# A two-block layer of convolution, token mix and channel mix: the token mix's sums taken for two blocks per instruction, with h1's columns reordered

## Chip, core and metric

One core of a Trainium2 chip runs the whole program. The metric is device time in microseconds (us) of one execution; the kernel before took 2136.81 us (median of two executions, 2135.29 and 2138.33).

## What is computed

```python
# x: 8 x 4096 x 192; weight: 8 heads x 7 taps
w = softmax(weight)                                     # over the 7 taps
xc[b, s, h, :] = sum_k w[h, k] * x[b, s + k - 6, h, :]   # causal convolution, 24 channels per head
h = relu(xc^T @ w_tok1) @ w_tok2                         # token mix: 4096 -> 256 -> 4096
u = xc + h^T
out = u + relu(u @ w_ch1) @ w_ch2                        # channel mix: 192 -> 1536 -> 192
```

All of it is float32 in and out. The matrix products are made of a high and a low part of each operand (three products per pair).

## The kernel before

The eight batches are taken in groups: batch 0, batch 1, and then three pairs (2,3), (4,5), (6,7). Each group has two stages. Stage 1 makes the convolution on ScalarE (first tap) and VectorE (other taps, line 667) and the first token product on TensorE, summed in PSUM; `mix1_done` (line 380) turns that sum into `h1`, the high part by ScalarE and the low part by VectorE. Stage 1 of a later group runs as background work: a planner (`Background`) keeps its own estimates of TensorE's and VectorE's time, and at every `bg.fg(pe, dve, after)` call in the foreground it places background instructions until its estimate for VectorE is `after` ns ahead of TensorE's. So the numbers given to `bg.fg` decide where taps stand on VectorE.

Stage 2 of a pair runs in units. A unit is one block of 512 tokens of both batches, that is two tiles, and there are eight units per pair, 24 in all. In the second tile of a unit the order on TensorE is: `channel1` (line 1077, six pairs of banks, evicted by line 1091 on ScalarE and line 1092 on VectorE), then `mix2` for the next unit (line 904), then the two halves of `channel2` (line 1119), then `channel1` of the next unit's first tile.

`mix2` for a pair makes four token blocks (`j` 0 to 3). Each is six matmuls of 384 columns (lines 930 to 932, h1's two batches of 192 columns side by side) into one bank of PSUM. Two blocks share one tile `two` of two banks; `banks()` hands out three such tiles in turn. After each block one VectorE add (line 936) reads the bank in u's order of columns (`p c b d`: block of 64 channels, batch, channel), while h1 has them as `b c d`, and adds it into `u`. Line 962 then transposes the block of `u` in 32x32 squares (`turn_blocks`). When all four blocks are turned, `blocks_sent` sends them to other partitions by 16 small DMAs (line 998, half on SyncE's queue and half on GpSimd's); then `release` lets the held background transfers go. `parted` splits what arrived into high and low (line 1011 ScalarE, line 1013 VectorE) and copies halves across (line 1016 ScalarE, line 1018 DMA). The next `channel1` reads these.

For batch 0's first tile `mix2` runs with `at_once`: four blocks of 18 small matmuls over both parts (lines 923 to 925), an add (line 942) and a copy (line 943) per block; here, too, two blocks share one two-bank tile. Batch 1 and the rest of batch 0 take the path of lines 927 and 953, which already adds two blocks at once.

Of the kernel before, what the change touches and what calls it, by code (L numbers as in the profile page):

```python
# [11 lines left out]
AF = mybir.ActivationFunctionType  # L12
ALU = mybir.AluOpType
# [126 lines left out]
def conv_mixer_kernel(ctx: ExitStack, tc: tile.TileContext, x, weight, w_tok1, w_tok2, w_ch1, w_ch2, out):  # L140
    nc = tc.nc
    B, S, D = x.shape
# [8 lines left out]
    D2 = P // 2  # L151
# [15 lines left out]
    def f32(ap):  # L167
        return ap.bitcast(F32)
# [7 lines left out]
    bg = Background()  # L176

    def banks():
        return ps_x.tile([P, 2, TT], F32, name="ps_x")
# [200 lines left out]
    def mix1_done(gi, accs):  # L380
        n = len(GROUPS[gi]) * D
        for kc in range(KC):
            a = accs[kc][:, :n]
            nc.scalar.activation(out=h1[:, kc, 0, :n], in_=a, func=AF.Relu)
            nc.vector.scalar_tensor_tensor(
                out=h1[:, kc, 1, :n], in0=a, scalar=0.0, in1=f32(h1[:, kc, 0, :n]), op0=ALU.max, op1=ALU.subtract
            )

    def mix1_accs():
        return [ps_a.tile([P, TT], F32, name=f"ps_a{kc}") for kc in range(KC)]  # L390
# [3 lines left out]
    def stage1_first(pe, p0, pd, late, load_u, load_next, after, thirds, hooks):  # L394
# [181 lines left out]
        for n in range(nj - 1):  # L576
# [10 lines left out]
            if n + 2 == nj:  # L587
                woven(chains[0][:1], chains[1][:1], split(n - 2))
                mix1_done(0, accs)
                woven(chains[0][1:])  # L590
                begin(n + 1)
                continue
# [39 lines left out]
    def stage1(gi, pools):  # L632
# [216 lines left out]
        def finish():  # L849
            bg.finish(gi)  # L850
            mix1_done(gi, accs)
# [44 lines left out]
    def rows(v):  # L896
        if len(v.shape) == 3:
            return v.rearrange("p j (c d) -> p j c d", d=D2)
        return v.rearrange("p (c d) -> p c d", d=D2)
# [4 lines left out]
    def mix2(gi, q, t2, u, at_once=False, turned=None, between=(), i=None):  # L904
        nb = len(GROUPS[gi])
        n = nb * D

        def lhs(kc, r, j):
            if gi:
                return t2[kc][:, r, j, :]  # L910
            a0 = ((q % 2) * TJ + j) * P
            return t2s[q // 2][:, kc, r, a0:a0 + P]

        for j in range(TJ):
            if j % 2 == 0:
                two = banks()
            ps = two[:, j % 2]
            for kc in range(KC):
                a, z = kc == 0, kc == KC - 1
                wh, wl = lhs(kc, 0, j), lhs(kc, 1, j)  # L920
                hh, hl = h1[:, kc, 0, :n], h1[:, kc, 1, :n]
                if at_once:
                    nc.tensor.matmul(out=ps[:, :D], lhsT=wh, rhs=hh, start=a, stop=False)
                    nc.tensor.matmul(out=ps[:, :D], lhsT=wh, rhs=hl, start=False, stop=False)
                    nc.tensor.matmul(out=ps[:, :D], lhsT=wl, rhs=hh, start=False, stop=z)
                elif nb == 1:
                    nc.tensor.matmul(out=ps[:, :2 * D], lhsT=wh, rhs=h1[:, kc, :, :n], start=a, stop=False)
                    nc.tensor.matmul(out=ps[:, :D], lhsT=wl, rhs=hh, start=False, stop=z)
                else:
                    nc.tensor.matmul(out=ps[:, :n], lhsT=wh, rhs=hh, start=a, stop=False)  # L930
                    nc.tensor.matmul(out=ps[:, :n], lhsT=wh, rhs=hl, start=False, stop=False)  # L931
                    nc.tensor.matmul(out=ps[:, :n], lhsT=wl, rhs=hh, start=False, stop=z)  # L932
            if nb > 1:
                bg.fg(1040, 532, 200)
                v = ps[:, :n].rearrange("p (b c d) -> p c b d", b=nb, d=D2)
                nc.vector.tensor_tensor(out=u[:, j], in0=v, in1=u[:, j], op=ALU.add)  # L936
                turn_blocks(u[:, j], turned, j)
                continue
            if at_once:
                bg.fg(570, 355, 200)  # L940
                one, two_ = u[:, j, :, 1], u[:, j, :, 0]
                nc.vector.tensor_tensor(out=two_, in0=rows(ps[:, :D]), in1=one, op=ALU.add)
                nc.scalar.copy(out=one, in_=two_)
                if j < len(between):
                    between[j]()
                continue
            bg.fg(570, 1110 if j % 2 else 0, 200)
            if j % 2 == 0:
                continue
            js = slice(j - 1, j + 1)  # L950
            one = u[:, js, :, 1 if i is None else i]
            total = u[:, js, :, 0] if i is None else one
            nc.vector.tensor_tensor(out=one, in0=rows(two[:, :, :D]), in1=one, op=ALU.add)
            nc.vector.tensor_tensor(out=total, in0=rows(two[:, :, D:2 * D]), in1=one, op=ALU.add)
            if i is None:
                nc.scalar.copy(out=one, in_=total)
            elif turned is not None:
                for k in (j - 1, j):
                    turn_blocks(u[:, k], turned, k)

    def turn_blocks(uj, turned, j):
        nc.vector.transpose(  # L962
            out=turned[:, :, j * QB:(j + 1) * QB],
            in_=uj.rearrange("p c b d -> p (c b d)").rearrange("p (n e) -> p n e", e=QB),
        )
        bg.dve += 580
# [69 lines left out]
    def first_mix(between):  # L1036
        mix2(0, 0, *first["u"], at_once=True, between=between)
# [206 lines left out]
    u = None  # L1244
# [9 lines left out]
    for gi, bs in enumerate(GROUPS):  # L1254
        nb = len(bs)
# [9 lines left out]
        if gi == 0:  # L1265
            u, abc = first["u"][1], first["abc"]
            loaded = first["next"]
        for n, unit in enumerate(units[gi]):
            nxt = (gi, n + 1) if n + 1 < len(units[gi]) else (gi + 1, 0)
            for i, (b, q) in enumerate(unit):  # L1270
# [27 lines left out]
                if turn and blocks:  # L1298
                    z = up.tile([P, ND * NQ, P], F32, name="own_hi")
                    t2, v = loaded  # L1300
                    if tiles:
                        for k in range(2 - len(t2), 2):
                            mix2(nxt[0], following[k][1], t2[k - 2], v, i=k, turned=z if k else None)
                    else:
                        mix2(nxt[0], nxt[1], t2[0], v, turned=z)
                    other = blocks_sent(z)
                    bg.release()
                elif turn:
                    if gi == 0 and nxt[0] == 0:
                        bg.require(("t2", nxt[1] // 2, nxt[1] % 2))  # L1310
                    mix2(*nxt, None, loaded[1])
                    mixed[0] = nxt[1]
                elif blocks and nxt[0] == gi and len(bs) == 1:
                    mix2(gi, following[0][1], loaded[0][0], loaded[1], i=0)
                    loaded = [load_t2(following[1][1], sp)], loaded[1]
# [27 lines left out]
                if turn:  # L1343
                    u = loaded[1]
# [33 lines left out]
```

## Time and profile before

| | |
|---|---|
| median of the two executions shown | 2136.81 us |
| the profiled execution | 2134.78 us, of which the span is 2133.0 us |
| TensorE busy | 2039.9 us (96%) |
| VectorE busy | 1410.8 us (66%) |
| ScalarE busy | 729.6 us (34%) |
| chain that ended last | 79% TensorE, 11% VectorE, 4% ScalarE |

The first unit's `mix2` for a pair begins at 610 us of the span, the last one's at 2056 us. In the names of the rows PE is TensorE's matmuls, PEld its weight loads, DVE VectorE, ACT ScalarE, POOL GpSimd, SP SyncE's queue. Matmuls overlap, so the distance from one start to the next is what one costs.

### The profile page before, as it was taken

How to read it: one execution, taken by the hardware profiler on the slowest of the kernel's cores; microseconds unless marked ns; L12 is line 12 of the kernel's file. 1: busy time of each engine (PE TensorE's matmuls, PEld its weight loads, DVE VectorE, ACT ScalarE, POOL GpSimd, SP SyncE). 2: the span in 40 equal slices, each digit the busy share in tenths (PEclk: the TensorE clock that was granted, in tenths of full speed). 3: DMA queues.
4: the chain of work that ended last, by engine and by line, in shares of the span. 5: the costliest groups of instructions: out<-in, count | busy, mean ns of one | idle time of the engine just before them, and what ended most of it. 6: DMA issues, size and time to landing. Idle time of an engine off the chain costs nothing.

```text
span 2133.0 us, 40820 instructions
## 1 busy us (share of the span) xinstructions
PE 2039.9 (96%) x17339; PEld 1868.5 (88%) x17339; DVE 1410.8 (66%) x2279; ACT 729.6 (34%) x863; POOL 240.9 (11%) x423
## 2 busy tenths in 40 slices
PE   9889999999999997999999999999999999999999
PEld 9779998899888897989888988998888889888788
DVE  7689876789858886856875689444445554445444
ACT  4564533334332332323333324223222232223222
POOL 0100001111111011101111110111110001111110
PEclk9999999999999999999999999999999999999999
DMA  9744537568454467234654334432221223223310
GB/s 316 253 144 153 172 105 193 160 180 230 115 175 113 138 177 192 78 90 132 161 148 115 96 107 136 139 82 80 80 62 53 59 74 80 80 73 80 80 38 23
DMA packets 294469, 264.61 MB, mean 124 GB/s; under 512 B 210512, under 2 KB 242768, under 8 KB 294288
## 3 DMA queue, kind: packets, MB, share of 16 engines
q1 hardware_dynamic: 268704, 169.57, 28.6%
q0 software_dynamic: 25584, 92.43, 14.5%
q8 instruction: 137, 2.24, 0.5%
q14 instruction: 44, 0.36, 0.1%
HBM read 146.60 MB, written 71.30 MB: 102 GB/s over the span
## 4 chain that ended last, share of the span: by engine, by line
PE 79%; DVE 11%; ACT 4%; issue 3%; DMA 2%; SPq 1%; POOL 0%; ACTq 0%; DVEq 0%; POOLq 0%
PE ps_x L1049 33%; PE ps_x L1108 15%; PE ps_x L1126 14%; PE ps_x L1127 6%; DVE xc L667 3%; DVE hl L1092 2%; ACT hh L1091 2%; PE ps_x L930 2%; DVE u L936 2%; PE ps_a L769 1%; PE ps_a L770 1%; PE ps_a L771 1%; PE ps_x L932 1%; PE ps_x L931 1%; PE ps_a L455 1%
## 5 line engine op out<-in xcount | busy, mean ns | idle before, releaser
L1091 ACT ACTIVATE hh<-ps_x 128x1024 fp32r<-128x1024 f32 x378 | 387.6, 1027 | 753.6 <-PE ps_x L1049 753.5
L1092 DVE SCALAR_TENSOR_TENSOR hl<-ps_x,hh 128x1024 fp32r<-128x1024 f32 x378 | 462.4, 1224 | 254.1 <-ACT hh L1091 253.1
L1126 PE MATMUL ps_x<-w,hh 128*128 128x384 f32 x1872 | 537.7, 359 | 6.8 <-DVE osb L1134 4.7
L1049 PE MATMUL ps_x<-other,w_hi 64*128 64x512 f32 x2016 | 533.1, 393 | 3.8 <-ACT other L1016 3.8
L1127 PE MATMUL ps_x<-w,hl 128*128 128x192 f32 x1872 | 468.5, 250 | 0.0
L1049 PEld LDWEIGHTS ps_x<-other,w_hi 64*128 64x128 f32 x2016 | 370.9, 186 | 42.2 <-ACT other L1016 4.9
L667 DVE SCALAR_TENSOR_TENSOR xc<-raw,cw,xc 128x384 f32<-128x384 f32 (+1 forms) x768 | 387.2, 562 | 17.6 <-ACT xc L665 17.5
L1126 PEld LDWEIGHTS ps_x<-w,hh 128*128 128x128 f32 x1872 | 351.3, 188 | 9.9 <-issue 4.7
L1127 PEld LDWEIGHTS ps_x<-w,hl 128*128 128x128 f32 x1872 | 357.4, 191 | 0.0
L1049 PE MATMUL ps_x<-own_hi,w_hi 64*128 64x512 f32 x1296 | 336.0, 398 | 21.6 <-DVE osb L1134 11.3
L1108 PE MATMUL ps_x<-w,hh 64*128 64x384 f32 x2304 | 329.5, 355 | 0.0
L1049 PE MATMUL ps_x<-own_hi,w_lo 64*128 64x512 f32 x1296 | 328.0, 391 | 0.0
L1049 PE MATMUL ps_x<-own_lo,w_hi 64*128 64x512 f32 x1296 | 327.2, 390 | 0.0
L1108 PE MATMUL ps_x<-w,hl 64*128 64x192 f32 x2304 | 292.7, 247 | 0.0
L1049 PE MATMUL ps_x<-other,w_lo 64*128 64x512 f32 x1008 | 285.4, 390 | 0.0
L1049 PEld LDWEIGHTS ps_x<-own_hi,w_hi 64*128 64x128 f32 x1296 | 212.1, 188 | 51.0 <-issue 16.0
L1049 PEld LDWEIGHTS ps_x<-own_hi,w_lo 64*128 64x128 f32 x1296 | 217.5, 187 | 23.8
L1049 PEld LDWEIGHTS ps_x<-own_lo,w_hi 64*128 64x128 f32 x1296 | 216.6, 187 | 23.3
L1108 PEld LDWEIGHTS ps_x<-w,hl 64*128 64x128 f32 x2304 | 226.0, 188 | 1.4 <-DVE hl L1092 0.5
L1108 PEld LDWEIGHTS ps_x<-w,hh 64*128 64x128 f32 x2304 | 221.9, 184 | 0.9
L1049 PEld LDWEIGHTS ps_x<-other,w_lo 64*128 64x128 f32 x1008 | 188.0, 187 | 19.5
L998 POOL DMA_DIRECT2D other<-own_hi x224 | 121.7, 551 | 540.4 <-DVE own_hi L962 395.6
(147 smaller groups left out, 2060.4 us busy)
## 6 DMA issues: line engine op xcount, KB each, us to landing
raw<-in_x_dram SPq DMA_DIRECT2D x56, 672.0 KB, 7.2
t<-t2d SPq DMA_DIRECT2D x62, 512.0 KB, 5.4
out_dram<-osb POOLq DMA_DIRECT2D x63, 384.0 KB, 4.3
u<-xcd SPq DMA_DIRECT2D x62, 384.0 KB, 6.7
xcd<-xc POOLq DMA_DIRECT2D x28, 768.0 KB, 7.5
t<-t1p SPq DMA_DIRECT2D x32, 512.0 KB, 4.9
other<-own_hi SPq DMA_DIRECT2D x224, 48.0 KB, 2.2
other<-own_hi POOLq DMA_DIRECT2D x224, 48.0 KB, 2.0
```

The costliest lines, as they stand in the source:

```text
L455: nc.tensor.matmul(out=accs[kc][:, :D], lhsT=tops[i][:, c0:c0 + P], rhs=xcs[j // NC][:, j % NC], start=j == 0, stop=j == NJ - 1,)
L667: nc.vector.scalar_tensor_tensor(out=dst, in0=src, scalar=cw[:, h, k:k + 1], in1=dst, op0=ALU.mult, op1=ALU.add)
L769: nc.tensor.matmul(out=ps, lhsT=wh, rhs=xh, start=a, stop=False)
L930: nc.tensor.matmul(out=ps[:, :n], lhsT=wh, rhs=hh, start=a, stop=False)
L936: nc.vector.tensor_tensor(out=u[:, j], in0=v, in1=u[:, j], op=ALU.add)
L998: queue.dma_start(out=f32(other[q * QB:(q + 1) * QB, 1, :, i * P:(i + 1) * P]), in_=blocks[i * QB:(i + 1) * QB, q])
L1049: nc.tensor.matmul(out=two[:, h], lhsT=w1[w][rows, c, p * P:(p + 1) * P], rhs=t[h][v][rows, c], start=n == 0, stop=n == len(prods) - 1,)
L1091: nc.scalar.activation(out=hh, in_=two, func=AF.Relu)
L1092: nc.vector.scalar_tensor_tensor(out=hl, in0=two, scalar=0.0, in1=f32(hh), op0=ALU.max, op1=ALU.subtract)
L1108: nc.tensor.matmul(out=ps[:, :m], lhsT=h[part, f][ks, ts], rhs=w2[ks, f, :m], start=n == 0 and part == "hh", stop=z and part == "hl",)
L1126: nc.tensor.matmul(out=ps[:, :2 * D], lhsT=h["hh", f][:, ts], rhs=w2[:, f, :], start=n == 0, stop=False)
L1127: nc.tensor.matmul(out=ps[:, :D], lhsT=h["hl", f][:, ts], rhs=w2[:, f, :D], start=False, stop=z)
```

## The change

Three things are edited. `mix1_done` writes h1 of a pair with its columns in u's order (block of 64 channels, batch, channel), in two instructions of 192 columns per bank and engine in place of one of 384. `mix2` of a pair adds and turns only after the second block of a two-bank tile: one add of 768 columns over both banks, then two transposes; the numbers given to the planner change with it (0 after an even block, 955 after an odd one, in place of 532 after each). And in the first tile each of the four blocks gets a two-bank tile of its own, of which it uses one bank.

```diff
     def mix1_done(gi, accs):
         n = len(GROUPS[gi]) * D
         for kc in range(KC):
-            a = accs[kc][:, :n]
-            nc.scalar.activation(out=h1[:, kc, 0, :n], in_=a, func=AF.Relu)
-            nc.vector.scalar_tensor_tensor(
-                out=h1[:, kc, 1, :n], in0=a, scalar=0.0, in1=f32(h1[:, kc, 0, :n]), op0=ALU.max, op1=ALU.subtract
-            )
+            parts = [(accs[kc][:, :n], h1[:, kc, 0, :n], h1[:, kc, 1, :n])]
+            if n > D:
+                a, hi, lo = parts[0]
+                a = a.rearrange("p (b c d) -> p b c d", b=2, d=D2)
+                hi, lo = (v.rearrange("p (c b d) -> p b c d", b=2, d=D2) for v in (hi, lo))
+                parts = [(a[:, i], hi[:, i], lo[:, i]) for i in range(2)]
+            for a, hi, lo in parts:
+                nc.scalar.activation(out=hi, in_=a, func=AF.Relu)
+                nc.vector.scalar_tensor_tensor(out=lo, in0=a, scalar=0.0, in1=f32(hi), op0=ALU.max, op1=ALU.subtract)
...
         for j in range(TJ):
-            if j % 2 == 0:
+            if j % 2 == 0 or at_once:
                 two = banks()
-            ps = two[:, j % 2]
+            ps = two[:, 0 if at_once else j % 2]
...
+            js = slice(j - 1, j + 1)
             if nb > 1:
-                bg.fg(1040, 532, 200)
-                v = ps[:, :n].rearrange("p (b c d) -> p c b d", b=nb, d=D2)
-                nc.vector.tensor_tensor(out=u[:, j], in0=v, in1=u[:, j], op=ALU.add)
-                turn_blocks(u[:, j], turned, j)
+                bg.fg(1040, 955 if j % 2 else 0, 200)
+                if j % 2:
+                    v = u[:, js].rearrange("p j c b d -> p j (c b d)")
+                    nc.vector.tensor_tensor(out=v, in0=two[:, :, :n], in1=v, op=ALU.add)
+                    for k in (j - 1, j):
+                        turn_blocks(u[:, k], turned, k)
                 continue
```

Place one, TensorE's rows in the first pair's first unit, with the semaphores that each waits for: the end of block 0, block 1, and the first row of block 2. Before:

```order
L931 MATMUL ps_x<-h_476,t_5911 128x384
L932 MATMUL ps_x<-h_476,t_5911 128x384
L930 MATMUL ps_x<-h_476,t_5911 128x384 [waits DVE_49]
L931 MATMUL ps_x<-h_476,t_5911 128x384
L932 MATMUL ps_x<-h_476,t_5911 128x384
L930 MATMUL ps_x<-h_476,t_5911 128x384
L931 MATMUL ps_x<-h_476,t_5911 128x384
L932 MATMUL ps_x<-h_476,t_5911 128x384
L930 MATMUL ps_x<-h_476,t_5911 128x384 [waits PE_49]
```

Now, where lines 934 to 936 are the same three matmuls:

```order
L935 MATMUL ps_x<-h_476,t_5917 128x384
L936 MATMUL ps_x<-h_476,t_5917 128x384
L934 MATMUL ps_x<-h_476,t_5917 128x384
L935 MATMUL ps_x<-h_476,t_5917 128x384
L936 MATMUL ps_x<-h_476,t_5917 128x384
L934 MATMUL ps_x<-h_476,t_5917 128x384
L935 MATMUL ps_x<-h_476,t_5917 128x384
L936 MATMUL ps_x<-h_476,t_5917 128x384
L934 MATMUL ps_x<-h_476,t_5917 128x384 [waits DVE_49]
```

The wait for VectorE at the head of block 1 is gone (block 3 has lost its own in the same way); the one at the head of block 2 is for the tile's earlier reader, the fifth eviction of `channel1` (line 1092 before, 1098 now). The matmuls and their order are the same.

Place two, VectorE's rows in the first pair's fourth unit, where background taps (line 667, now 671) stand among the adds. Before:

```order
L1092 SCALAR_TENSOR_TENSOR hl_8130<-ps_x,hh_8129 128x1024 x2
L667 SCALAR_TENSOR_TENSOR xc_7735<-raw_7720,cw,xc_7735 128x16x24 x4
L936 TENSOR_TENSOR u<-ps_x,u 128x384
L962 STREAM_TRANSPOSE own_hi<-u 128x12x32
L667 SCALAR_TENSOR_TENSOR xc_7735<-raw_7720,cw,xc_7735 128x16x24 x2
L936 TENSOR_TENSOR u<-ps_x,u 128x384
L962 STREAM_TRANSPOSE own_hi<-u 128x12x32
L936 TENSOR_TENSOR u<-ps_x,u 128x384
L962 STREAM_TRANSPOSE own_hi<-u 128x12x32
L936 TENSOR_TENSOR u<-ps_x,u 128x384
L962 STREAM_TRANSPOSE own_hi<-u 128x12x32
L667 SCALAR_TENSOR_TENSOR xc_7735<-raw_7720,cw,xc_7735 128x16x24 x4
```

Now:

```order
L1098 SCALAR_TENSOR_TENSOR hl_8130<-ps_x,hh_8129 128x1024 x2
L671 SCALAR_TENSOR_TENSOR xc_7735<-raw_7720,cw,xc_7735 128x16x24 x8
L942 TENSOR_TENSOR u<-ps_x,u 128x768
L968 STREAM_TRANSPOSE own_hi<-u 128x12x32 x2
L942 TENSOR_TENSOR u<-ps_x,u 128x768
L968 STREAM_TRANSPOSE own_hi<-u 128x12x32 x2
L671 SCALAR_TENSOR_TENSOR xc_7735<-raw_7720,cw,xc_7735 128x16x24 x4
```

Four adds became two, and eight taps instead of four stand ahead of the first. Eight of the 24 units now have 2 to 8 taps there (two of these eight had 4 before, three had 2, three none); in the other 16 nothing stands between the last eviction and the first add, as before.

Place three, SyncE's queue behind the sends of that same unit: `raw` are background loads of x, `t<-t1p` loads of the first token weight. Before:

```order
L655 DMA raw_8356<-in_x_dram 128x14x96 x2
L727 DMA t_8453<-t1p 128x1024
L655 DMA raw_8455<-in_x_dram 128x14x96 x2
L727 DMA t_8492<-t1p 128x1024
L880 DMA t_8538<-t2d 128x2x512 x2
```

Now:

```order
L659 DMA raw_8356<-in_x_dram 128x14x96 x2
L659 DMA raw_8430<-in_x_dram 128x14x96 x2
L731 DMA t_8476<-t1p 128x1024
L731 DMA t_8498<-t1p 128x1024
L884 DMA t_8535<-t2d 128x2x512 x2
```

The second pair of x loads moved ahead of the first weight load. It is the one place where the queues of SyncE and GpSimd differ.

## Rows read from the trace of the kernel before

**Rows 1.** The page: engine busy time, and the chain's shares.
```profile
PE 2039.9 (96%) x17339; PEld 1868.5 (88%) x17339; DVE 1410.8 (66%) x2279; ACT 729.6 (34%) x863; POOL 240.9 (11%) x423
PE 79%; DVE 11%; ACT 4%; issue 3%; DMA 2%; SPq 1%; POOL 0%; ACTq 0%; DVEq 0%; POOLq 0%
```
**Rows 2.** Groups by line and form: count | busy us, mean ns | idle before.
```profile
L1092 DVE SCALAR_TENSOR_TENSOR hl<-ps_x,hh 128x1024 fp32r<-128x1024 f32 x378 | 462.4, 1224 | 254.1 <-ACT hh L1091 253.1
...
L930 PE MATMUL ps_x<-h,t 128*128 128x384 f32 x192 | 73.4, 382 | 47.6 <-DVE u L936 47.6
...
L936 DVE TENSOR_TENSOR u<-ps_x,u 128x384 f32<-128x384 f32 x96 | 52.8, 550 | 50.7 <-PE ps_x L932 50.7
...
L753 DVE TENSOR_TENSOR xhl<-xc,xhl 128x768 fp32r<-128x768 f32 x48 | 45.4, 945 | 6.8 <-ACT xhl L749 6.8
...
L930 PEld LDWEIGHTS ps_x<-h,t 128*128 128x128 f32 x192 | 36.8, 192 | 70.7 <-DVE u L936 62.2 <-issue 7.4 <-DVE xc L667 1.1
...
L923 PE MATMUL ps_x<-h,t2s 128*128 128x192 f32 x8 | 2.9, 358 | 3.1 <-DVE u L942 3.0
...
L384 ACT ACTIVATE h<-ps_a 128x192 fp32r<-128x192 f32 x4 | 1.2, 340 | 5.6 <-PE ps_a L455 5.6
```
**Rows 3.** The waits: who waited for whom, us in total, times, longest.
```profile
PE ps_x L930 <- DVE u L936: 47.6, 45, 1.8
```
**Rows 4.** TensorE's timeline in a unit at 1457 us: start, us, instruction, idle before.
```profile
1457.35 0.44 PE L930 MATMUL ps_x<-h,t 128*128 128x384 f32 x1
...
1460.29 0.44 PE L930 MATMUL ps_x<-h,t 128*128 128x384 f32 x1 [1.62 <-DVE u L936]
...
1461.46 0.33 PE L930 MATMUL ps_x<-h,t 128*128 128x384 f32 x1
...
1462.33 0.34 PE L932 MATMUL ps_x<-h,t 128*128 128x384 f32 x1
1463.33 0.44 PE L930 MATMUL ps_x<-h,t 128*128 128x384 f32 x1 [0.66 <-DVE u L936]
...
1464.50 0.33 PE L1126 MATMUL ps_x<-w,hh 128*128 128x384 f32 x1
```
**Rows 5.** VectorE's timeline in the same unit.
```profile
1458.54 1.23 DVE L1092 SCALAR_TENSOR_TENSOR hl<-ps_x,hh 128x1024 fp32r<-128x1024 f32 x1 [0.84 <-ACT hh L1091]
1459.68 0.55 DVE L936 TENSOR_TENSOR u<-ps_x,u 128x384 f32<-128x384 f32 x1
1460.27 0.58 DVE L962 STREAM_TRANSPOSE own_hi<-u 128x384 f32<-128x384 f32 x1
...
1464.70 0.56 DVE L936 TENSOR_TENSOR u<-ps_x,u 128x384 f32<-128x384 f32 x1 [0.81 <-PE ps_x L932]
1465.29 0.58 DVE L962 STREAM_TRANSPOSE own_hi<-u 128x384 f32<-128x384 f32 x1
```
**Rows 6.** ScalarE's timeline: the copy that channel1 needs, first unit and this unit.
```profile
629.38 1.48 ACT L1016 CAST other<-own_hi 64x1536 fp32r<-64x1536 f32 x1
...
1474.84 1.47 ACT L1016 CAST other<-own_hi 64x1536 fp32r<-64x1536 f32 x1
```
**Rows 7.** TensorE's timeline: channel1's first matmul that reads the copy, same two units.
```profile
631.36 0.49 PE L1049 MATMUL ps_x<-other,w_hi 64*128 64x512 f32 x1
...
1478.22 0.49 PE L1049 MATMUL ps_x<-other,w_hi 64*128 64x512 f32 x1
```
**Rows 8.** TensorE's timeline: three waits inside channel1, in three units.
```profile
766.87 0.46 PE L1049 MATMUL ps_x<-own_hi,w_hi 64*128 64x512 f32 x1 [2.27 <-DVE osb L1134]
...
844.80 0.76 PE L1049 MATMUL ps_x<-own_hi,w_hi 64*128 64x512 f32 x1 [8.47 <-DVE osb L1134]
...
2016.18 0.50 PE L1049 MATMUL ps_x<-other,w_hi 64*128 64x512 f32 x1 [2.04 <-ACT other L1016]
```
**Rows 9.** VectorE's timeline ahead of the middle one of these waits.
```profile
838.40 3.27 DVE L667 SCALAR_TENSOR_TENSOR xc<-raw,cw,xc 128x384 f32<-128x384 f32 x6 [8.64 <-ACT xc L665]
```
**Rows 10.** Busy time and granted clock around the mix at 1990 us.
```profile
1990.00:1999.00 9.00, 6.73 (x30) 5.55 (x27) 5.36 (x8) 1.03 (x1) 0.00 (x0) 0.81 0.00 0
```

More of the change, by code (lines that the diff above doesn't have):

```diff
@@ L949, in mix2 @@
                 continue
-            js = slice(j - 1, j + 1)
             one = u[:, js, :, 1 if i is None else i]
```

## The prediction

> **What bounds the kernel now.** I read the page first: TensorE is busy 96% of the span and holds 79% of the chain that ended last; VectorE has 66% and 11% [rows 1]. So a change pays only where TensorE stands still, and the next view is the one of groups with the idle time before each. The pair's token mix, line 930, stands out: 47.6 us of idle time, all of it ended by line 936, VectorE's add [rows 2]. The waits count it: 45 times, 1.8 us at the longest [rows 3]. There are 24 mixes with two two-bank tiles each, so 48 places, one per tile.
>
> The timeline of one mix shows where. The matmul at 1460.29 is the first of block 1: it stood 1.62 us until the add of block 0. The one at 1463.33 is the first of block 3 and stood 0.66 us for the add of block 2 [rows 4]. Block 2, in another tile, did not wait. TensorE writes the second bank of a tile while VectorE reads the first one; the program guards the tile as a whole. The first wait is longer because the add of block 0 had to follow the last eviction of channel1, which ran from 1458.54 to 1459.77, before it could run at 1459.68 [rows 5].
>
> **The change part by part.** *The waits removed.* In the order of the changed kernel no matmul of a pair's mix waits for an add any more; blocks 0 and 2 wait for evictions of channel1, which are earlier. What one wait costs is more than its idle time. This mix took 1464.50 - 1457.35 = 7.15 us; in its undisturbed part five steps take 0.87 us, so one is 0.174 us and 24 are 4.18 [rows 4]. Of the 2.97 us more, 0.1 is the slow first matmul, which stays (0.44 in place of 0.33 us), 2.28 is idle time, and some 0.6, 0.3 per wait, is the restart behind it. For 45 waits: 47.6 + 45 x 0.3 = 61.1 us. The weight loads of the same line give the same from the other side: 62.2 us idle for the add [rows 2]. Bounds: 47.6, if the restart is hidden, and 62.2.
>
> *One add of 768 columns over two banks, twice, for four of 384.* The trace has no such add. The nearest rows are 768 elements from SBUF, 945 ns, and an eviction of 1024 over two banks, 1224 ns; two of the old adds are 1100 [rows 2]. I take 950 ns, as the first has the size and a plain add of 384 from PSUM (550) differs from what that size would give by little. VectorE does 96 x 0.55 - 48 x 0.95 = 7 us less, which is off the path and counts nothing.
>
> *What is late next: the sends.* The last transpose of a unit releases the small DMAs, and at their far end channel1 waits for line 1016. Before, the last transpose ended at 1465.87, 1.37 us after channel2 had begun [rows 4, 5]. Now the first add can again start at about 1459.7; with 0.95 us and two transposes at a 0.5 us step, VectorE is free near 1461.7, and TensorE ends its 24 matmuls at 1457.35 + 0.1 + 4.18 = 1461.6. The second add and its two transposes take 0.95 + 0.5 + 0.6 = 2.1 us, to 1463.8, and channel2 begins at 1461.6: 2.2 us instead of 1.37. The sends come 2 us earlier in time but 0.85 us later against TensorE. The cover is the slack in front of channel1: the copy ended at 1476.3 and was read at 1478.22, 1.9 us; in the first unit 630.86 against 631.36, 0.5 us [rows 6, 7]. The same subtraction over the 24 units gives 0.5 to 6 us, except for the unit at 2016 us, which waited 2.04 already [rows 8]. So 0.35 comes back in the first unit, 0.85 at 2016, and where the planner now puts two more taps ahead of the first add (three units without background matmuls, 2 x 0.53 us more) about 0.5 in all; 0.3 for the rest. Sum 2 us. If the cover were gone everywhere it would be 24 x 0.85 = 20 us.
>
> *The taps ahead of the adds.* In five other units 4 to 8 taps stand ahead of the first add, up to 8 x 0.53 = 4.2 us. In these, 24 background matmuls stand inside the mix, another 24 x 0.174 = 4.2 us of TensorE's work, so the adds end about as far behind as above. Channel2's first half needs the last eviction, which the taps follow and which ends 1.8 us before channel2 would begin (1459.77 against 1461.6); its second half needs the first add, some 7 us later. Nothing.
>
> *Two units that end on background work.* At 766.87 and 844.80 channel1 waits 2.27 and 8.47 us for an add of channel2 that stands behind taps [rows 8], and those stood 8.64 us for data [rows 9]. That data is fetched only after the sends, so these waits end 2 us earlier and not 2.9: 0.9 us lost in each, 1.8 us. Loads that SyncE now issues in another order at this place follow the first ones, whose data the taps wait for; I count nothing, and 5 us either way in the range.
>
> *First tile.* Line 923 waits 3.1 us for adds [rows 2]; a bank pair per block ends that, but what follows is a chain of decoding. I take 1 of 0 to 3 us. *h1's columns.* 12 more small instructions over the kernel, 6 on each of ScalarE and VectorE, in place of the longer halves, at 0.34 us [rows 2]; hidden by the twelve us of channel1 that run before the mix reads h1. Uncovered, at most 12 x 0.34 = 4 us.
>
> **The sum**, against the profiled execution, 2134.8: - 61.1 (waits) - 1 (first tile) + 2 (sends) + 1.8 (background) = 2076.5. The median of the runs shown is 2 us above that execution, so I forecast 2078 us.
>
> One thing could give more. Around the mix at 1990 us the granted clock is 0.81 over 9 us [rows 10], so TensorE spent a good third of them at 1.2 and not 2.4 GHz; just before, the engine had stood still twice. One other mix shows the same. If these losses go with the stalls, it is 3 us less. The Trainium skill (TensorE: Matmul & The Clock Gate, "A second HAM failure mode: psum-queue depth-cycling") says that short idle stretches between groups of matmuls can make the clock fall again and again; the trace agrees only in part, as 22 of the 24 mixes with the same stalls ran at the full clock.
>
> **Rivals.** *The late sends eat it.* The larger add and the paired transposes push the next channel1 back in every unit, not in five. For it: in one unit that wait exists already [rows 8]. Against: 1.9 us of slack where 0.85 are taken [rows 6, 7]. It would give 24 x 0.85 = 20 in place of 2 us: 2097 us. The Trainium skill (Perfetto Trace Analysis, "Optimizing Scalar/DVE Operations") speaks for this rival: where VectorE isn't saturated but makes other engines wait, smaller instructions let work end sooner, and this change makes them larger. By the rows the small ones are what TensorE waited for, since each guarded a whole tile.
>
> *The first pair's units are bound by background work.* VectorE's taps and the loads behind the sends set the pace at 730 to 950 us, and what is taken out of the mixes there comes back as longer waits like those at 766 and 844 [rows 8, 9]. At 2.9 us for each of four units, 12 us don't come: 2090 us. Against: between 610 and 730, and from 882 on, channel1 shows no such wait.
>
> *The waits move (no change).* If VectorE were late, not the guard, TensorE would meet the eviction one step later. That decides if the last eviction ends over 4.2 us after the mix begins; it ends 2.4 us after [rows 4, 5]. 2135 us.
>
> *Slower.* Eight units have taps ahead of the adds. If a tap there waits for x, as it did for 8.64 us once [rows 9], the adds, the transposes and the sends stand behind it on VectorE, and channel2's second half waits for its bank. From 7.6 us in each of the eight this outweighs the 61; at 8.64 it is 2078 + 69 = 2147 us. Against: where the planner put taps there before, the adds were late by no more than 1.8 us [rows 3].
>
> **How the numbers follow.** The forecast has 0.74, the background rival 0.12, late sends 0.08, moved waits 0.04, slower 0.02. The range runs from 2066 (the clock's 3, the first tile's 2 more, no loss of 4, and 3 of the queue's order) to 2095, which takes in the background rival and all but the end of the late sends, and holds 0.86. About 2% can be told from no change here; that line is 2094 us. Faster than that: the forecast and the background rival, 0.86. Within 2%: late sends and moved waits, 0.12. Slower: 0.02.
>
> **What would show it.** In the changed kernel's profile the first matmul of a mix should have no idle time ended by the add; a mix of a late unit should last 4.3 us, and 7.15 no more; the step from one unit to the next should fall by 2.9 us from 1457 us on; the new add should take 0.95 us; the idle time for line 1016's successor should rise by some 2 us. Idle time of that line in most units, or of channel1 for adds of channel2 beyond 14 us, would make the forecast wrong; so would taps with idle time before them right ahead of an add.

## The result, and the profile after

The changed kernel took 2074.88 us (median of two executions, 2072.74 and 2077.01) against 2136.81 us: a ratio of 0.971, with a 95% interval of 0.966 to 0.976. The forecast was 2078 us. In a later series, five rounds beside the kernel before, the changed kernel stood at 2076.82 us and 0.972 (0.970 to 0.974); in a last one at 2075.66 us and 0.972 (0.970 to 0.973).

The prediction's sum was made between profiled executions, so it is compared with them: 2134.78 us before, 2077.01 us after, 57.8 us less where the sum said 58.3.

The page of the changed kernel, engine busy time and the chain's shares, to be held against [rows 1]:

```profile
PE 2027.0 (98%) x17339; PEld 1877.1 (90%) x17339; DVE 1400.3 (67%) x2237; ACT 730.5 (35%) x869; POOL 241.2 (12%) x423
...
PE 81%; DVE 9%; ACT 3%; DMA 3%; issue 2%; SPq 1%; POOL 0%; ACTq 0%; POOLq 0%; DVEq 0%
```

TensorE runs the same 17339 matmuls and is busy 12.9 us less; VectorE is busy 10.5 us less, 42 instructions fewer. The groups by line and form (count | busy us, mean ns | idle before), against [rows 2]; lines 934 to 936 are the old 930 to 932, line 942 the old 936, line 927 the old 923:

```profile
L934 PE MATMUL ps_x<-h,t 128*128 128x384 f32 x192 | 67.0, 349 | 0.0
L942 DVE TENSOR_TENSOR u<-ps_x,u 128x768 f32<-128x768 f32 x48 | 45.8, 954 | 16.2 <-PE ps_x L936 15.5
L934 PEld LDWEIGHTS ps_x<-h,t 128*128 128x128 f32 x192 | 36.0, 188 | 8.5 <-issue 7.8 <-DVE xc L671 0.7
L927 PE MATMUL ps_x<-h,t2s 128*128 128x192 f32 x8 | 2.4, 299 | 0.1
```

The 47.6 us of idle time at the mix's first matmuls are 0.0, and of the 62.2 us that its weight loads waited for the add nothing is left; the matmul's mean fell from 382 to 349 ns. The new add takes 954 ns. The timelines of a late unit with no background matmuls show the rest: TensorE first (start, us, instruction; lines 1055 and 1132 are the old 1049 and 1126), from the mix's first matmul past channel2's first to the next mix, against [rows 4, 7]:

```profile
1430.02 0.44 PE L934 MATMUL ps_x<-h,t 128*128 128x384 f32 x1
...
1434.30 0.33 PE L1132 MATMUL ps_x<-w,hh 128*128 128x384 f32 x1
...
1448.03 0.49 PE L1055 MATMUL ps_x<-other,w_hi 64*128 64x512 f32 x1
...
1486.40 0.44 PE L934 MATMUL ps_x<-h,t 128*128 128x384 f32 x1
```

VectorE in the same mix, against [rows 5] (line 1098 is the last eviction of channel1, line 968 the transposes):

```profile
1431.21 1.23 DVE L1098 SCALAR_TENSOR_TENSOR hl<-ps_x,hh 128x1024 fp32r<-128x1024 f32 x1 [0.84 <-ACT hh L1097]
1432.42 0.96 DVE L942 TENSOR_TENSOR u<-ps_x,u 128x768 f32<-128x768 f32 x1
1433.41 1.04 DVE L968 STREAM_TRANSPOSE own_hi<-u 128x384 f32<-128x384 f32 x2
1434.50 0.96 DVE L942 TENSOR_TENSOR u<-ps_x,u 128x768 f32<-128x768 f32 x1
1435.49 1.04 DVE L968 STREAM_TRANSPOSE own_hi<-u 128x384 f32<-128x384 f32 x2
```

The mix lasts 1434.30 - 1430.02 = 4.28 us where it lasted 7.15, and the step to the next unit is 1486.40 - 1430.02 = 56.38 us; before, two such units began at 1457.35 and 1516.60, a step of 59.25. ScalarE's copy (line 1022, the old 1016) of the first unit, with channel1's first read of it there, and of the same late unit, against [rows 6, 7]:

```profile
627.11 1.47 ACT L1022 CAST other<-own_hi 64x1536 fp32r<-64x1536 f32 x1
...
628.64 0.50 PE L1055 MATMUL ps_x<-other,w_hi 64*128 64x512 f32 x1
...
1445.45 1.48 ACT L1022 CAST other<-own_hi 64x1536 fp32r<-64x1536 f32 x1
```

The copy ends at 1446.93 and channel1 reads it at 1448.03: 1.1 us of slack are left of the 1.9. In the first unit it ends at 628.58, and channel1 starts on it at 628.64: no slack is left there.

### The profile page after: what moved, and what is told of

The parts are those of the page before. It is cut to its first block, busy times and chain, and to the rows that moved or that the text cites. A ratio compares the mean times of both kernels' runs of the same rounds, so it can differ in the third digit from the quotient of the medians.

```text
span 2075.2 us, 40759 instructions
## 1 busy us (share of the span) xinstructions
PE 2027.0 (98%) x17339; PEld 1877.1 (90%) x17339; DVE 1400.3 (67%) x2237; ACT 730.5 (35%) x869; POOL 241.2 (12%) x423
## 4 chain that ended last, share of the span: by engine, by line
PE 81%; DVE 9%; ACT 3%; DMA 3%; issue 2%; SPq 1%; POOL 0%; ACTq 0%; POOLq 0%; DVEq 0%
PE ps_x L1055 34%; PE ps_x L1114 15%; PE ps_x L1132 14%; PE ps_x L1133 6%; DVE xc L671 3%; PE ps_x L934 2%; DVE hl L1098 2%; PE ps_x L936 2%; PE ps_x L935 2%; PE ps_a L773 1%; PE ps_a L774 1%; PE ps_a L775 1%; DMA raw<-in_x_dram 1%; PE ps_a L459 1%; SPq L1004 1%
## 5 line engine op out<-in xcount | busy, mean ns | idle before, releaser
L1114 PEld LDWEIGHTS ps_x<-w,hl 64*128 64x128 f32 x2304 | 231.8, 188 | 2.1 <-DVE hl L1098 1.3
L1114 PEld LDWEIGHTS ps_x<-w,hh 64*128 64x128 f32 x2304 | 228.0, 184 | 0.9
```

Of the source, the lines that this page charges most:

```text
L1114: nc.tensor.matmul(out=ps[:, :m], lhsT=h[part, f][ks, ts], rhs=w2[ks, f, :m], start=n == 0 and part == "hh", stop=z and part == "hl",)
```

## The experiments

Two theories were set against each other. By the first, TensorE waited because the program guards a two-bank tile as a whole, so any layout in which a matmul's tile is not the one an add reads takes the waits away; what limits the gain after that is how late the sends leave. By the second, the size, number or access order of the adds is what counts. The changed kernel has three edits (first tile, h1's column order with a plain add, one add for two blocks) and they were taken apart first, each against the kernel before.

**h1's order alone**, with one add per block as before:

```diff
+                v = u[:, j].rearrange("p c b d -> p (c b d)")
+                nc.vector.tensor_tensor(out=v, in0=ps[:, :n], in1=v, op=ALU.add)
```

> The kernel before with h1's columns in u's order and so a plain, contiguous add, but one add of 384 per block and two blocks in one tile as before. Guard theory: the waits stay, 2137 us, within 3 us of before. Layout rival (reading the bank in its own order makes the add shorter, or frees TensorE or VectorE): 2076 to 2110 us.

It took 2137.08 us, a ratio of 0.9998 (0.998 to 1.001). The groups of this kernel:

```profile
L934 PE MATMUL ps_x<-h,t 128*128 128x384 f32 x192 | 73.3, 382 | 47.6 <-DVE u L940 47.6
L940 DVE TENSOR_TENSOR u<-ps_x,u 128x384 f32<-128x384 f32 x96 | 52.7, 549 | 52.0 <-PE ps_x L936 52.0
```

TensorE's idle time is that of [rows 2], and the add takes 549 ns where it took 550: the order of the columns is worth nothing by itself that can be told, within 4 us by the interval, and the twelve more small instructions cost nothing that can be told either.

**One tile per block**, with the adds of the kernel before, unchanged in size and order:

```diff
-            if j % 2 == 0:
+            if j % 2 == 0 or nb > 1:
                 two = banks()
-            ps = two[:, j % 2]
+            ps = two[:, 0 if nb > 1 else j % 2]
```

> The kernel before, with h1's columns, the four adds of 384 columns and the planner's numbers as they were; only that each of the pair's four blocks gets a two-bank tile of its own and uses one bank of it. Guard theory: no matmul waits for the add of the block ahead of it, so most of the gain comes without larger adds; block 2's tile is now the one whose last eviction ends 2.4 us after the mix begins and it would start at 2.1, so some 0.65 us are lost in the 15 mixes without background matmuls: 2076 + 10 - 3 (sends as early as before the change) = 2083 us, 2075 to 2090. Work rival (the gain comes from fewer or plainer instructions on VectorE): 2135 us.

It took 2081.85 us, 0.9745 (0.9718 to 0.9771). TensorE's timeline in a unit at 1437 us, and VectorE's:

```profile
1437.34 0.44 PE L930 MATMUL ps_x<-h,t 128*128 128x384 f32 x1
...
1439.82 0.44 PE L930 MATMUL ps_x<-h,t 128*128 128x384 f32 x1
...
1442.04 0.33 PE L1126 MATMUL ps_x<-w,hh 128*128 128x384 f32 x1
```

```profile
1438.54 1.23 DVE L1092 SCALAR_TENSOR_TENSOR hl<-ps_x,hh 128x1024 fp32r<-128x1024 f32 x1 [0.84 <-ACT hh L1091]
1439.68 0.55 DVE L936 TENSOR_TENSOR u<-ps_x,u 128x384 f32<-128x384 f32 x1
...
1440.77 0.52 DVE L936 TENSOR_TENSOR u<-ps_x,u 128x384 f32<-128x384 f32 x1
```

The adds are as small as before, yet the mix lasts 4.70 us and not 7.15. So the guard on the tile was the cause. Blocks 1 and 2 run on while VectorE is still at block 0. The planner's numbers are the old ones here, and the background taps stand among the adds where they stood before, so the gain does not come from new places for them. This agrees with the Trainium skill (PSUM — Partial Sum Buffer, "PSUM bank collisions raise a hardware error"), which asks for a guard per bank and quadrant of partitions: the two blocks were in different banks all along, and only the program's tile joined them. What is left, 0.4 us a mix against the changed kernel in the 16 mixes without background matmuls, stands ahead of block 2, at 1439.82: with four tiles used in a mix and not two, that block already needs the tile that channel1's last eviction gives back at 1439.77 (1438.54 + 1.23), as was expected.

**The merged add alone**, with h1's old order (and two adds of 384 columns over both banks), without the first tile's edit:

```diff
+                if j % 2:
+                    js = slice(j - 1, j + 1)
+                    for m in range(nb):
+                        v = u[:, js, :, m]
+                        nc.vector.tensor_tensor(out=v, in0=rows(two[:, :, m * D:(m + 1) * D]), in1=v, op=ALU.add)
+                    for k in (j - 1, j):
+                        turn_blocks(u[:, k], turned, k)
```

> The kernel before with the adds taken after the second block of a tile, over both banks, but h1's columns as before: two adds of 384 (one per batch, over both banks) in place of one of 768. Guard theory: the waits are gone, and the pair of adds takes 0.2 us more than one of 768 would: 2077 us, 2072 to 2082. Layout rival: not below 2110 us. Late-sends rival: the tail is 0.2 us longer than in the changed kernel, so 5 us or more above it.

It took 2079.97 us, 0.9728 (0.970 to 0.9756). Its groups, and VectorE's timeline for the first two blocks of a mix:

```profile
L939 DVE TENSOR_TENSOR u<-ps_x,u 128x384 f32<-128x384 f32 x96 | 48.8, 550 | 15.2 <-PE ps_x L932 15.1
```

```profile
1434.22 1.02 DVE L939 TENSOR_TENSOR u<-ps_x,u 128x384 f32<-128x384 f32 x2
1435.28 1.04 DVE L966 STREAM_TRANSPOSE own_hi<-u 128x384 f32<-128x384 f32 x2
```

Its mixes last 4.29 us, as in the changed kernel. Two adds of 384 take 1.02 us together and the one of 768 takes 0.96; the 0.2 us expected between them are 0.06. Whether the sums are made in 96 instructions or in 48 hardly counts, and the interval holds the changed kernel. All of the large gain is in when an add is issued relative to the matmuls that share its tile.

**The first tile's edit alone**, on the kernel before:

```diff
-            if j % 2 == 0:
+            if j % 2 == 0 or at_once:
                 two = banks()
-            ps = two[:, j % 2]
+            ps = two[:, 0 if at_once else j % 2]
```

> The kernel before with the edit of the first tile alone: each of its four blocks has a two-bank tile of its own. Guard theory (the gain is the waits of the pairs' mix for the tile that is being read): the 24 mixes are as before, so 2136 us, within 2 us of the kernel before; the 3.1 us of line 923's waits go, but what follows is a chain of decoding. First-tile rival (part of the 58 us comes from a start that is earlier): 2100 us or less.

It took 2131.3 us, 0.9976 (0.9961 to 0.9992): 5 us less, by the interval 2 to 8, where the prediction had 1 and the expectation no more than 2. That was tested again from the other side, the changed kernel with these two lines put back, beside the changed kernel itself in one series.

> The changed kernel with line 919 as it was before: the first tile's mix takes its four blocks two to a two-bank tile again; everything else of the change stays. Prediction's size for the first tile (1 us, 0 to 3): 2077 to 2079 us, 1 above the changed kernel in the same series, idle time of about 3 us back in the first tile's mix. Rival, as the run of the first-tile edit alone suggests (2 to 8 us): 2079 to 2085 us, 5 above the changed kernel.

> The changed kernel once more, for the comparison with the one without the first tile's edit: 2076.5 us, as in the series before. Its mixes without idle time, the step between two late units 56.4 us.

They took 2077.42 (0.9725, 0.971 to 0.9741) and 2075.66 us (0.9719, 0.9703 to 0.9734): the edit is worth 1.8 us by the medians, and the intervals overlap. Both kernels have their place in the trace; first the kernel before, then the changed one, TensorE in the first tile (line 981, 987 after, is the transposes that follow; a block here is six matmuls, 24 in all, not the 18 per block of the description ahead):

```profile
57.45 0.39 PE L923 MATMUL ps_x<-h,t2s 128*128 128x192 f32 x1
...
59.83 0.36 PE L923 MATMUL ps_x<-h,t2s 128*128 128x192 f32 x1 [0.80 <-DVE u L942]
...
63.56 0.53 PE L923 MATMUL ps_x<-h,t2s 128*128 128x192 f32 x1 [2.16 <-DVE u L942]
...
68.43 1.65 PE L1049 MATMUL ps_x<-own_hi,w_hi 64*128 64x512 f32 x6 [0.25 <-ACT own_hi L984]
```

```profile
59.97 0.39 PE L927 MATMUL ps_x<-h,t2s 128*128 128x192 f32 x1
...
65.85 1.47 PE L987 MATMUL ps_x<-ident,u 128*128 128x128 f32 x10 [2.05 <-ACT u L950]
67.98 1.65 PE L1055 MATMUL ps_x<-own_hi,w_hi 64*128 64x512 f32 x6 [0.67 <-ACT own_hi L990]
```

From the mix's first matmul to channel1 it was 10.98 us and is 8.01, a gain of 3 us, though a new wait of 2.05 us for the copies stands there. (In the other profiles with the edit it is 8.0 to 8.6 us.) In the two profiled executions the first mix of a pair begins at 610.48 before and 610.55 after, as if nothing had come through, but the changed one began its first tile 2.5 us later (59.97 against 57.45). That start varies without the edit (57.4 to 61.1 us) as with it (58.4 to 61.2). So the distance from the first tile's first matmul to the first mix of a pair is the fairer measure: 553.0 to 555.3 us in the five profiled kernels with the old tiles, 549.2 to 552.1 in the seven with the new ones, 3.5 us less by the means. The whole gain of about 3 us is kept that far, and both comparisons of times allow 3.

**The sends, later still.** The changed kernel with the last two transposes of each unit made twice, which holds the sends back by another 0.9 us and leaves TensorE's work as it is:

```diff
+                if j == 3:
+                    said = bg.dve
+                    for k in (2, 3):
+                        turn_blocks(u[:, k], turned, k)
+                    bg.dve = said
```

> The changed kernel with the last two transposes of every unit made twice, which holds the sends back by about another 1.0 us. Theory (slack in front of channel1 of 0 to 1.1 us is left in the units without background matmuls, 2 us and more in most others): summed over the units with the slack measured in the changed kernel, 10 us more, 2085 us. Rival, no slack: 24 us more, 2099 us. Rival, slack of over 1 us everywhere: no change.

It took 2088.79 us, 0.9776 (0.9759 to 0.9793), 12 us above the changed kernel in the same series. ScalarE's copy in a late unit, then TensorE: two waits inside channel1 and the first read of that copy.

```profile
1455.83 1.48 ACT L1027 CAST other<-own_hi 64x1536 fp32r<-64x1536 f32 x1
```

```profile
761.69 0.54 PE L1060 MATMUL ps_x<-own_hi,w_hi 64*128 64x512 f32 x1 [4.03 <-DVE osb L1145]
...
839.62 0.76 PE L1060 MATMUL ps_x<-own_hi,w_hi 64*128 64x512 f32 x1 [11.31 <-DVE osb L1145]
...
1457.43 0.49 PE L1060 MATMUL ps_x<-other,w_hi 64*128 64x512 f32 x1
```

The copy ends at 1457.31 and is read at 1457.43: the slack is down to 0.1 us, and the step to the next unit, from 1439.42 to 1495.83, is still 56.41 us. In eleven of the units without background matmuls the slack ran out and the step grew against the changed kernel's, by 0.15 to 1.2 us and in one unit by 3.8; both background waits grew as well. So the first 0.9 us of lateness, the change's own, was mostly covered, and the next 0.9 costs 12 us of the 22 that 24 units without any cover would pay. This is the late-sends rival's price, one step further on than it stood.

**A shorter tail.** The changed kernel with blocks 2 and 3 in tiles of their own and added one at a time, so that the last add is the small one:

```diff
+            alone = at_once or nb > 1 and j > 1
-            if j % 2 == 0 or at_once:
+            if j % 2 == 0 or alone:
...
+                if j > 1:
+                    v = u[:, j].rearrange("p c b d -> p (c b d)")
+                    nc.vector.tensor_tensor(out=v, in0=ps[:, :n], in1=v, op=ALU.add)
+                    turn_blocks(u[:, j], turned, j)
```

> The changed kernel, but blocks 2 and 3 have a two-bank tile each and are added and turned one by one, so that the last transpose ends 1.37 us after channel2's start again and not 2.23. Theory (the late sends cost 0.85 us where the slack in front of channel1 is gone, and in the two units that end on background loads, elsewhere nothing): 3 us less than the changed kernel, 2072 us, within 2068 to 2075. If the sends' delay costs nothing: the same as the changed kernel. If it costs in every unit: 20 us less, 2055 us.

It took 2075.08 us, 0.9715 (0.9696 to 0.9734): no gain. VectorE in a late unit:

```profile
1428.41 1.23 DVE L1103 SCALAR_TENSOR_TENSOR hl<-ps_x,hh 128x1024 fp32r<-128x1024 f32 x1 [0.84 <-ACT hh L1102]
1429.62 0.96 DVE L947 TENSOR_TENSOR u<-ps_x,u 128x768 f32<-128x768 f32 x1
1430.61 1.04 DVE L973 STREAM_TRANSPOSE own_hi<-u 128x384 f32<-128x384 f32 x2
1431.57 0.52 DVE L943 TENSOR_TENSOR u<-ps_x,u 128x384 f32<-128x384 f32 x1
...
1433.17 0.58 DVE L973 STREAM_TRANSPOSE own_hi<-u 128x384 f32<-128x384 f32 x1
```

In the 16 units without background matmuls the edit did not do what it was made for. From the end of the last eviction VectorE works without a pause for 4.1 us however the adds are cut, and channel2 begins at 1431.50, so the transposes end 2.25 us after it, as in the changed kernel. The tail there is VectorE's queue behind that eviction, not the size of the last add. In five of the eight units with background matmuls the tail did fall from 2.23 to 1.38 us; in four of the five VectorE stands and waits for TensorE ahead of the last two adds, so it has no queue there. But these had 2 us of slack and more already, so nothing was to be won.

**The planner's number.** The changed kernel with the old figures for the foreground, which moves some taps, though not back to where they stood: three units lose the two taps ahead of their first add, one has six in place of eight, and the others are as in the changed kernel:

```diff
-                bg.fg(1040, 955 if j % 2 else 0, 200)
+                bg.fg(1040, 532, 200)
```

> The changed kernel with the planner's old numbers (532 after each block), so that background taps stand elsewhere among the adds. Guard theory: the same waits are gone, 2075 us, within 3 us of the changed kernel. Planner rival (the new places of the taps carry part of the gain, or cost part of it): 5 us or more to either side.

It took 2075.04 us, 0.9716 (0.9696 to 0.9735), beside the changed kernel, once more, in the same series.

> The changed kernel again, as the measure for the other three: 2075 us, 2072 to 2078.

The latter took 2076.82 us. In the kernel with the old figures all 24 tails are 2.23 us; in the changed one three are 3.0, from the two taps ahead of the first add, and one is 2.5. That is no difference in the time that can be told. The run tests only this small move; that the gain does not need the taps' new places is shown by the one with a tile per block. Neither this version nor the one before it beats the changed kernel by more than the measurement's width.

## Why the prediction was right, point by point

**The waits: 61.1 forecast, 60.5 found.** Taking for all 24 mixes the time from the first matmul to channel2's first, the sum was 199.7 us and is 136.2 (16 mixes of 4.29 us and eight of 8.45 with 24 background matmuls): 63.5 less, of which 3.0 belong to two mixes that ran in part at half the clock before. The part of the term that rested on reasoning, 0.3 us of restart per wait, is confirmed by itself: in each of the other 22 mixes the time that went is the idle time and 0.28 to 0.30 us more per wait (in the one of [rows 4], 2.87 us of which 2.28 were idle). Over 45 waits that is 12.9 us. Between the first mix and the last, by engine (us, busy us of PE, PEld, DVE, ACT and POOL with counts, granted clock, DMA share and rate), first the kernel before, then the changed one:

```profile
609.00:2058.00 1449.00, 1389.62 (x12548) 1266.87 (x12544) 890.91 (x1411) 448.38 (x493) 169.60 (x300) 0.99 0.38 103
```

```profile
609.00:2003.00 1394.00, 1376.53 (x12554) 1271.81 (x12551) 880.31 (x1369) 448.71 (x497) 169.58 (x300) 0.99 0.40 107
```

TensorE's busy time fell by 13.1 us there with nearly the same matmuls. That this is so close to 45 x 0.3 is chance: in the mixes alone it fell by 63.5 - 47.6 = 15.9 us, 12.9 of restart and 3.0 of clock, and some 3 us were added outside them. So a wait cost 1.06 us of idle time and 0.29 us more that the profile books as work, and the lower bound of 47.6 us would have been a fifth too small.

**The new add: 0.95 us forecast, 0.954 measured.** VectorE's saving of 7 us (52.8 to 45.8) was off the path.

**The late sends: 2 us forecast, 1.5 found.** The tail went from 1.37 to 2.23 us, 2.2 forecast. The slack in a late unit fell by 0.8, to 1.1 us. The steps lose 0.06, 0.22 and 0.30 us in the changed kernel's units at 610, 1599 and 1881 us, where the slack had run out, and 0.95 in the unit that had waited already. TensorE's four waits inside channel1 in the changed kernel, against [rows 8] (line 1017, the old 1011, is the copy of what was received, line 1140 the old 1134), and under them the wait at the copy of line 1011 before:

```profile
758.21 0.76 PE L1055 MATMUL ps_x<-own_hi,w_hi 64*128 64x512 f32 x1 [3.75 <-DVE osb L1140]
...
835.24 0.76 PE L1055 MATMUL ps_x<-own_hi,w_hi 64*128 64x512 f32 x1 [9.21 <-DVE osb L1140]
...
1957.78 0.50 PE L1055 MATMUL ps_x<-own_hi,w_hi 64*128 64x512 f32 x1 [1.68 <-ACT own_hi L1017]
1960.32 0.79 PE L1055 MATMUL ps_x<-other,w_hi 64*128 64x512 f32 x1 [2.04 <-ACT other L1022]
```

```profile
2013.64 0.50 PE L1049 MATMUL ps_x<-own_hi,w_hi 64*128 64x512 f32 x1 [0.73 <-ACT own_hi L1011]
```

One sign that the prediction gave was wrong: the idle time of the copy's own wait did not rise by 2 us, it stayed at 2.04. The loss stands one instruction earlier, at the copy of what the DMA brought in (1.68 us, against 0.73 before), since everything behind the sends is late together.

**The two background units: 1.8 us forecast, 1.7 to 2.8 found.** Their waits are 3.75 and 9.21 us in place of 2.27 and 8.47, as VectorE's taps stand for data that follows the sends (against [rows 9]):

```profile
829.71 4.32 DVE L671 SCALAR_TENSOR_TENSOR xc<-raw,cw,xc 128x384 f32<-128x384 f32 x8 [10.43 <-ACT xc L669]
```

The two mixes became 5.8 us shorter together and the two steps 3.1 us in this execution; in the two later profiles of the same kernel 4.0 and 4.1. The mechanism holds, and the size of the sum varies by 1 us from one execution to the next. The split into 0.9 and 0.9 is borne out only in the last of those (0.8 and 0.9, with waits of 3.22 and 9.25 us); in the execution shown it is 2.7 and 0.1.

The prediction named a limit here: more than 14 us of waits in channel1 for channel2's adds would make the forecast wrong. The waits, before and after (us in total, times, longest):

```profile
PE ps_x L1049 <- DVE osb L1134: 11.3, 3, 8.5
```

```profile
PE ps_x L1055 <- DVE osb L1140: 15.1, 3, 9.2
```

The limit was passed, also in the two later profiles (14.2 and 14.6), and the forecast stood: the limit was set too close. The third of these waits lies at 562 us, ahead of the pairs' first mix; it is 0.6 us before and 2.1 after. It is 2.1 us in the profiles of the own tiles, the merged add and h1's order as well and 0.5 us in those of the first tile's edit and of the planner's old number, so it goes with no one part of the change; what sets it stays open.

The rival that put 12 us on the four units of that stretch is refuted by the same sums: their mixes became 9.0 us shorter, their steps 5.7, so 3.2 us were given back.

**The first tile: 1 us forecast, about 3 found**, the term that was mis-sized. The row of waits (3.1 us) was the right one to read; that a chain of copies would take all but 1 of it back was a guess, and 3 us were left at its end. The 2 us that were added to the sum for the median had no ground: the changed kernel's median lies 2 us under its profiled execution, not above it.

**The clock: 3 us possible, 3.0 found in the mixes, little net.** The two mixes with a stretch at half the clock were real, 1.5 us longer each (8.65 against 7.13); the granted clock (0.50) in the first of them, before:

```profile
672.80:676.20 3.40, 3.40 (x11) 3.40 (x12) 1.57 (x3) 0.00 (x0) 0.00 (x0) 0.50 0.00 0
```

In the changed kernel no mix is slowed, and the other profiles bear that out. Of the three profiled kernels with the waits (before, h1's order alone, the first tile alone) two or three of the 24 mixes hold such a stretch, 8 of 72, each about 1.5 us longer for it; of the nine without the waits no mix does. So these losses do go with the stalls, as the prediction thought possible. But outside the mixes a stretch at 1.2 GHz behind a longer wait can be wider, as the one around the waits at 1957 and 1960 us, which was half as long before and is again half as long in the last profile of the changed kernel:

```profile
1958.90:1965.70 6.80, 5.38 (x26) 4.27 (x28) 1.86 (x5) 3.77 (x3) 1.64 (x3) 0.50 0.84 175
```

The core's span and mean granted clock, before and after:

```profile
core 0: 2133.0 us, clock 0.989
```

```profile
core 0: 2075.2 us, clock 0.988
```

A mean of 0.989 is 2 x 0.011 x 2133 = 47 us at half the clock, one of 0.988 is 50 us, each to some 2 us by the rounding; so no fall of the whole can be told from these two. By the Trainium skill (TensorE: Matmul & The Clock Gate, "A second HAM failure mode: psum-queue depth-cycling") frequent short idle stretches between groups of matmuls make the clock fall and rise again. The traces agree in part: 8 of 72 mixes with stalls lost clock and none without, but 64 with such stalls did not.

**The balance, and some luck.** 63.5 us out of the mixes, 57.8 out of the span. The 5.7 between them: 2.8 in the two background units, 1.8 in the unit with the waits at 1957 and 1960 us (0.95 of waiting; the rest goes with the longer stretch at the lower clock), 0.6 in three units that ran out of slack, 0.5 in a unit with background matmuls at 936 us (its cause is open). That 57.8 meets the sum's 58.3 so well is partly luck: the clock's 3.0 us, which the sum left out, stand against losses larger than forecast, and the first tile's 3 us, three times the forecast, do not show in this pair because the changed execution began its first tile 2.5 us later. The medians of the three series are 60.3 to 61.9 us apart, so the sum is rather 2 to 4 us short, and the 2 us added for the median made the forecast of 2078 us worse, not better.

The other rivals: had the waits moved to the eviction, the mix would have stayed near 7 us; and no tap between the last eviction and the first add had idle time before it, which the slower case needed.

## What to carry to other kernels

When TensorE waits for an engine that reads another bank than the one to be written, look at what the program's buffer covers before making the reader faster: reading both banks once, at the end, or giving each block its own buffer took the wait away (2080 and 2082 us), and reordering the data for a plainer add did nothing (2137 us). Count a removed wait at its idle time plus the slower restart behind it, and take off what the cover in front of the next wait lacks, unit by unit: here the slack was 1.9 us in a late unit and 0.5 to 6 in all but one, the first 0.9 us of lateness cost 1.5 us over the 24 units and about 2 more in the two that end on background work, and the next 0.9 us cost 12.

## What the runs showed that was not expected

A wait of 1.06 us took 1.35 us of TensorE's time, the last 0.3 booked as busy time of the matmuls and so invisible in a list of waits. An add of 768 columns over two banks costs 0.96 us and two of 384 columns cost 1.02 back to back, so the number of instructions hardly mattered for VectorE: the Trainium skill (Perfetto Trace Analysis, "Optimizing Scalar/DVE Operations") has smaller instructions let work end sooner when an unsaturated VectorE holds up other engines, and here cutting the last adds in two moved the end of VectorE's work by nothing (2.25 against 2.23 us behind channel2's start) in the 16 units where that engine was working without a pause in that stretch; in four units where it had a pause there the end moved from 2.23 to 1.38 us, as the Trainium skill has it. And the clock fell inside 8 of 72 mixes with stalls and inside none without, yet the whole time at half the clock, near 50 us, did not fall by an amount that can be told.
